# Talking-heads attention feeding a gated feed-forward on one core: two score tiles per step, and the last two batches' attention values kept in SBUF

## The chip, the cores and the metric

One core of a Trainium2 chip runs the whole program. The metric is device time in microseconds (us), the median of three executions; lower is better. Beside it stands one profiled execution, from which all durations below come.

## The reference, cut to what matters

```python
# attention: q, k, v are (4 batches, 12 heads, 448 tokens, 64), float32
scores = scale * np.matmul(q, k.transpose(0, 1, 3, 2))
scores = np.einsum('bhij,hg->bgij', scores, w_pre)        # heads mixed before the softmax
scores = scores - np.max(scores, axis=-1, keepdims=True)
attn = np.exp(scores)
attn = attn / (np.sum(attn, axis=-1, keepdims=True) + 1e-09)
attn = np.einsum('bhij,hg->bgij', attn, w_post)           # and after it
attn_out = np.matmul(attn, v)
# x is attn_out as (1792 tokens, 768); the feed-forward has d_ff = 1536
g = x @ w_gate
out = (g * (1.0 / (1.0 + np.exp(-g))) * (x @ w_val)) @ w_out
```

The three feed-forward weights come in as float64 and are turned into float32 on the chip.

## The kernel before, in words

**Stages.** The attention of batches 0 to 3 runs first, and the feed-forward after it in two halves: first the tokens of batches 2 and 3, then those of batches 0 and 1. For the second half the products of the two batches are combined from seven sums and differences of their values (`b11`, `t1`, `b21` and so on), which the attention of batch 1 makes (`second_values`, L379, with `operand`, L355) and stores in DRAM.

**Attention of a batch.** `load_k`, `kprep`, `kcopy` bring and transpose the keys, two heads at a time (six steps); `load_q`, `qprep`, `qcopy` the queries, 128 rows at a time (four chunks, two steps each). `qk` (L207) makes the scores of a group of head pairs, `qkcopy` (L220) copies them from PSUM to the tile `stg`, and `store` (L229) sends them to DRAM (`s_d`). There are 21 such groups in a batch: six for each of three chunks and three for the last. Rows are then worked in 45 tiles of ten query rows (`NTB`), two tiles making a unit (`NUB` = 23 units, the last with one tile). For each unit `gather` (L247) reads the scores of its rows back from DRAM with heads on the partitions, and `pre` (L264) mixes the heads into two PSUM banks, one for each tile. For each tile follow `top` (L276, row maximum, VectorE), `expo` (L282, exponential and row sum, ScalarE), `norm` (L288, reciprocal on VectorE, then the scaled mixing weights `rw` on GpSimd), `post` (L296, second mixing, eight matmuls) and `mixed` (L307, copy into the ring `attnT`, ScalarE). `av` (L317) multiplies by the values for two heads and two column chunks of 112 rows; `values` (L332) splits the result into a high and a low part (ScalarE copy, VectorE subtraction). For batches 2 and 3 both parts go to DRAM as `x_d`, and `load_x` and `load_last` (L667, L673) read them back into the two large tiles `x0`, `x1` before the feed-forward's first products (`up`, L679).

**PSUM.** The eight banks are four pairs: `qk`, `pre`, `post`, and `tr` for transposes and `av`. A `pre` bank is free again when its tile's `expo` has read it.

**Order.** It is written by hand. Every step is entered with `at(key, step)`, and `run` (L86) issues all steps in the order of their keys; each engine and each DMA queue works through its own steps in that order. A key counts tiles: batch b begins at `n0 = 45*b`, unit u at `n0 + 2*u`; I call the stretch of two tiles from there a slot. Nearly all DMAs go through the SP queue, which holds what is behind a DMA that still waits. From key 163.2 (`START`) the first three weight units are converted to float32 during the attention (`convert`, eight steps, seven of them on VectorE for these units), and the feed-forward's own keys start at `END` = 192.

```python
at(n + 0.5, later(pre, b, u))                          # L447, n = n0 + 2*u
n = n0 + t - x + 0.5                                   # L450, x = t % 2
at(n + 0.3 + 0.1 * x, later(top, b, t))
at(n + 0.9 + 0.4 * x, later(expo, b, t))
at(n + 1.6 + 0.4 * x, later(norm, b, t))
at(n + 2.7 + 0.8 * x, later(post, b, t))
at(n + 3.2 + 0.8 * x, later(mixed, b, t))
```

## Time and profile before

| what | us |
|---|---|
| median of three executions (1033.2 to 1205.98) | 1034.08 |
| the profiled execution | 1040.06 |
| its span, from first to last instruction | 1038.3 |
| TensorE busy (its matmuls) | 989.4 |
| VectorE busy | 670.3 |
| ScalarE busy | 432.5 |
| GpSimd busy | 229.5 |

The profile has a page with busy times, and views that answer questions: a timeline (start, duration, engine, line, operation, tile; in brackets the idle time of the engine in front of it and what ended it), a table of busy time by stretch, and a list of waits. PE is TensorE's matmuls, PEld its weight loads, DVE VectorE, ACT ScalarE, POOL GpSimd, SPq the DMAs that the SP queue issues. The ends of matmuls are modelled in these rows and overlap with the next ones, so what a step takes from TensorE is read here from the start of one group to the start of the next.

### The profile page before, as it was taken

The page shows a single profiled execution, that of the slowest core. Times are in us where ns is not written, and L with a number is a line of the kernel's source. Part 1 is how long each engine was busy: PE and PEld are TensorE (multiplying, and loading weights), DVE is VectorE, ACT ScalarE, POOL GpSimd, SP SyncE. Part 2 cuts the span into 40 slices and gives each one's busy share as a digit, 9 for nine tenths or more (in the row PEclk, how much of TensorE's full clock was granted, in tenths as well). Part 3 has the DMA queues.
Part 4 walks back from the last instruction along what each step waited for, and adds up shares of the span by engine and source line. Part 5 has one row for each costly group of instructions (what it writes and reads, how often), then busy time and mean ns, then how long its engine had stood idle before and what let it go on. Part 6 is the DMA issues. An engine that isn't in the chain of part 4 may idle for free.

```text
span 1038.3 us, 18515 instructions
## 1 busy us (share of the span) xinstructions
PE 989.4 (95%) x6732; PEld 770.9 (74%) x6732; DVE 670.3 (65%) x1336; ACT 432.5 (42%) x961; POOL 229.5 (22%) x278
## 2 busy tenths in 40 slices
PE   5899999989989999999969999999999999999998
PEld 2456556645545665556859999999999899999998
DVE  3466555656556655547459999999954999994110
ACT  1355555644545555555523333332313444442110
POOL 2011111101101111112223443344413333330000
PEclk9799999989999999999989999999999999999999
DMA  7789776987679965787745454557974111111311
GB/s 193 237 223 280 230 220 209 286 235 246 191 234 273 272 219 182 222 245 228 242 144 183 156 164 147 173 164 250 325 246 150 61 62 61 61 61 62 104 45 36
DMA packets 159318, 190.05 MB, mean 183 GB/s; under 512 B 56984, under 2 KB 134652, under 8 KB 159228
## 3 DMA queue, kind: packets, MB, share of 16 engines
q1 hardware_dynamic: 158972, 188.78, 59.7%
q8 instruction: 54, 0.88, 0.4%
q14 instruction: 36, 0.29, 0.1%
q0 software_dynamic: 256, 0.09, 0.0%
HBM read 114.10 MB, written 74.75 MB: 182 GB/s over the span
## 4 chain that ended last, share of the span: by engine, by line
PE 72%; DVE 14%; DMA 6%; ACT 3%; issue 2%; POOL 2%; SPq 1%; ACTq 0%; DVEq 0%; POOLq 0%
PE post L302 13%; PE pre L272 9%; PE qk L217 7%; PE av L324 6%; PE dn L721 6%; PE dn L722 6%; PE dn L723 6%; PE p L619 4%; PE p L622 4%; PE p L620 4%; DVE w L540 2%; DVE w L542 2%; DVE stg L225 1%; DVE wlo L558 1%; DMA raw<-in_moe_w_val_dram 1%
## 5 line engine op out<-in xcount | busy, mean ns | idle before, releaser
L302 PEld LDWEIGHTS post<-rw,e 128*112 128x112 f32 x1440 | 160.2, 179 | 83.8 <-issue 49.6
L302 PE MATMUL post<-rw,e 128*112 128x120 f32 (+1 forms) x1440 | 187.1, 277 | 5.9 <-POOL rw L293 5.3
L293 POOL TENSOR_SCALAR rw<-w_post_gs,st 128x120 f32<-128x120 f32 x180 | 69.1, 387 | 425.4 <-DVE st L291 249.4
L285 ACT ACTIVATE e<-pre,st 128x448 f32<-128x448 f32 x180 | 114.0, 633 | 97.2 <-DVE st L279 97.2
L279 DVE TENSOR_REDUCE st<-pre 128x1 f32<-128x448 f32 x180 | 105.0, 619 | 67.2 <-PE pre L272 62.5
L721 PE MATMUL dn<-whi,gh 128*128 128x256 f32 x504 | 141.6, 281 | 1.4 <-DVE u L626 1.4
L723 PE MATMUL dn<-whi,gl 128*128 128x256 f32 x504 | 141.5, 281 | 0.0
L722 PE MATMUL dn<-wlo,gh 128*128 128x256 f32 x504 | 141.4, 281 | 0.0
L530 POOL TENSOR_SCALAR mag<-mag 128x768 f32<-128x768 f32 x33 | 98.9, 2997 | 150.1 <-ACT mag L528 147.3
L272 PE MATMUL pre<-rs,w_pre_blocks 60*64 60x448 f32 x720 | 116.9, 581 | 15.3 <-ACT e L285 11.6
L311 ACT ACTIVATE attnT<-post 112x480 f32<-112x480 f32 (+3 forms) x192 | 103.1, 545 | 34.2 <-PE post L302 33.7
L721 PEld LDWEIGHTS dn<-whi,gh 128*128 128x128 f32 x504 | 95.0, 188 | 1.6 <-DVE u L626 1.6
L722 PEld LDWEIGHTS dn<-wlo,gh 128*128 128x128 f32 x504 | 95.0, 189 | 0.0
L723 PEld LDWEIGHTS dn<-whi,gl 128*128 128x128 f32 x504 | 95.0, 188 | 0.0
L225 DVE COPY stg<-qk 128x448 f32<-128x448 f32 x124 | 73.2, 618 | 27.4 <-PE qk L217 26.9
L217 PE MATMUL qk<-kk,qt 64*128 64x448 f32 (+1 forms) x384 | 89.9, 605 | 0.8 <-ACT stg L227 0.6
L324 PE MATMUL av<-attnT,vn 112*64 112x224 f32 (+1 forms) x864 | 84.9, 342 | 2.3 <-DVE xs L338 1.9
L324 PEld LDWEIGHTS av<-attnT,vn 112*64 112x64 f32 x864 | 54.6, 139 | 28.7 <-issue 8.3
L558 DVE TENSOR_TENSOR wlo<-w,whi 128x768 fp32r<-128x768 f32 x48 | 45.6, 952 | 30.5 <-ACT whi L562 30.2
L272 PEld LDWEIGHTS pre<-rs,w_pre_blocks 60*64 60x64 f32 x720 | 25.8, 133 | 51.6 <-ACT e L285 33.0
L686 PE MATMUL upg<-x,whi 128*128 128x448 f32 x144 | 54.2, 376 | 6.9 <-DMA x<-x_d 6.9
L562 ACT ACTIVATE whi<-w 128x768 fp32r<-128x768 f32 x48 | 40.1, 839 | 37.2 <-PE dn L723 21.6
(115 smaller groups left out, 1647.6 us busy)
## 6 DMA issues: line engine op xcount, KB each, us to landing
rs<-s_d SPq DMA_DIRECT2D x176, 210.0 KB, 4.4
s_d<-stg SPq DMA_DIRECT2D x72, 448.0 KB, 3.6
w_d<-w SPq DMA_DIRECT2D x36, 384.0 KB, 2.7
w<-w_d SPq DMA_DIRECT2D x36, 384.0 KB, 3.3
raw<-in_moe_w_gate_dram SPq DMA_DIRECT2D x12, 768.0 KB
raw<-in_moe_w_val_dram SPq DMA_DIRECT2D x12, 768.0 KB, 4.8
raw<-in_moe_w_out_dram SPq DMA_DIRECT2D x12, 768.0 KB, 5.5
kn<-in_k_dram SPq DMA_DIRECT2D x24, 224.0 KB, 5.7
```

The source lines that it names most:

```text
L217: nc.tensor.matmul(pt[x][i * m:(i + 1) * m], qt[b, c][hs, p, :m], kk[b, p][hs], start=True, stop=True)
L225: nc.vector.tensor_copy(stg[b, c, g][:, x], pt)
L272: nc.tensor.matmul(pt[r][x * HB:(x + 1) * HB], wpre[i], xs[i, x], start=True, stop=True)
L279: nc.vector.tensor_reduce(st[:, 0:1], pt, axis=AX.X, op=ALU.max, negate=True)
L285: nc.scalar.activation(e, pt, AF.Exp, bias=st[:, 0:1], scale=1.0, accum_out=st[:, 1:2])
L302: nc.tensor.matmul(pt[:, c, :, :m], e[:, c * CP:(c + 1) * CP], w[:, :, :m], start=True, stop=True)
L311: nc.scalar.activation(attnT[:, :, :, i:i + m].rearrange("p c h i -> p (c h) i"), pt[:, :, :, done:done + m].rearrange("p c h i -> p (c h) ...
L324: nc.tensor.matmul(pt[j * D:(j + 1) * D], vn[b][:, 2 * p + j, c], ring[:, c, 2 * p + j, segs[0]:segs[-1] + 1:max(1, segs[-1] - segs[0])], ...
L530: eng.tensor_scalar(mag, mag, f32_of(0x38000000), f32_of(0x47EFFFFF), op0=ALU.max, op1=ALU.min)
L721: nc.tensor.matmul(pt, gh, hi, start=opens, stop=False)
L722: nc.tensor.matmul(pt, gh, lo, start=False, stop=False)
L723: nc.tensor.matmul(pt, gl, hi, start=False, stop=closes)
```

## The change

1. **Two tiles together.** `top`, `expo`, `post`, `mixed` of the two tiles of a unit stand directly behind one another, both `expo` ahead of the `mixed` of the unit before, and `norm` works once for a unit: one addition and one reciprocal on two columns, then two `rw` on GpSimd. Both `post` (16 matmuls) stand together.
2. **All attention steps by slots.** One scoring group, with its copies and its store, stands in each slot; key and query preparation, `av`, `values` have fixed places in a slot. Of the second query chunk of batch 0 only the first group's products stand in front of the first `pre` (before, four groups did). In batch 0 both first query loads are entered behind the six key loads and ahead of the score stores.
3. **Batches 2 and 3 straight into SBUF.** `values` writes the high and low parts into `x0` and `x1`; `x_d`, its 30 stores and 16 loads go.
4. **Batch 1's sums.** The low parts of `t1` to `t4` and one subtraction move from VectorE to GpSimd (30 operations of 128x224), the steps stand later, and for the second pair later still. Buffers: `xs` 4 for 3, `x_b12` 2 for 1.
5. **Start of the feed-forward.** The whole first gate product and the first half of the first value product stand ahead of the last six `av`.

```diff
-    xsp = pool(right, "xsp", 3, "right")
+    xsp = pool(right, "xsp", 4, "right")
...
-        early_bank = b == 0 and c < 2 and g % 2 and g < 5
+        early_bank = b == c == 0 and g % 2 and g < 5
...
+    def norm(b, u):
+        n = len(tiles_of(u))
+        st = sts.pop((b, u))
+        nc.vector.tensor_scalar(st[:, 2, :n], st[:, 1, :n], 1e-9, None, op0=ALU.add)
+        nc.vector.reciprocal(st[:, 2, :n], st[:, 2, :n])
+        for r, t in enumerate(tiles_of(u)):
+            w = rw[b, t] = smp.tile([P, H, TS], F32, tag="rw", name=f"rw_{b}_{t}")
+            nc.gpsimd.tensor_scalar(w, wpost, st[:, 2, r:r + 1], 1.0, op0=ALU.mult, op1=ALU.mult)
...
         if b * S >= TB:
-            keep_x(x_d[:, p * P:(p + 1) * P, ts], xs, m)
+            if (0, 0) not in xs_:
+                for x in range(2):
+                    xs_[0, x] = stp.tile([P, NKC, TB], F32R, tag="stg", name=f"x{x}")
+            hi, lo = (xs_[0, x][:, p, ts].rearrange("p (s i) -> p s i", s=m) for x in range(2))
...
+            eng = nc.vector if order else nc.gpsimd
             for o, i in order or [(slice(None), slice(None))]:
-                nc.vector.tensor_tensor(xs[:, 1, i], src[:, o], xs[:, 0, i].bitcast(F32), op=ALU.subtract)
+                eng.tensor_tensor(xs[:, 1, i], src[:, o], xs[:, 0, i].bitcast(F32), op=ALU.subtract)
...
-            nc.vector.tensor_tensor(xt["b21", c], xt["b21", c], xt["t1"], op=ALU.subtract)
+            nc.gpsimd.tensor_tensor(xt["b21", c], xt["b21", c], xt["t1"], op=ALU.subtract)
...
+    BACK = 13
+        def slot(u):
+            return (n0 if u >= 0 else n0 - NTB) + 2 * (u if u >= 0 else u + NUB)
...
+            n = slot(BACK - 2 + p - NUB) if b else (-31.8 + 0.5 * p if p < 2 else -31.8 + p)
+            at(n - 4 if b else -60 + p, later(load_k, b, p))
+            at(n + 1.25, later(kprep, b, p))
+            at(n + 1.45, later(kcopy, b, p))
...
+            if b:
+                at_k = [slot(BACK - NUB + done + g) for g in range(len(groups(c)))]
+                ready = [slot(BACK - NUB + done - (4 if c == 0 else 2) + g) for g in range(2)]
+            elif c == 0:
+                at_k, ready = [-29.65 + g for g in range(NPAIR)], [-32.3, -30.8]
+            elif c == 1:
+                at_k, ready = [-1.0 + 1.2 * g for g in range(NPAIR)], [-5.0, -4.0]
             else:
+                at_k = [slot(done - 9 + g) for g in range(len(groups(c)))]
+                ready = [slot(done - 11 + g) for g in range(2)]
+            at(min(ready[0] - 8, -54 + c) if b == 0 and c < 2 else ready[0] - 8, later(load_q, b, c))
...
+            for g, n in enumerate(at_k):
+                at(n + 0.65, later(qk, b, c, g))
                 for x in range(2):
+                    at(n + (0.9 if x or g % 2 else 1.1), later(qkcopy, b, c, g, x))
+                at(n + 1.4, later(store, b, c, g))
+            done += len(at_k)
         for u in range(NUB):
+            n = slot(u)
+            at(n - 4.05, later(gather, b, u))
             at(n + 0.5, later(pre, b, u))
+            for t in tiles_of(u):
+                x = 0.02 * (t % 2)
+                at(n + 0.6 + x, later(top, b, t))
+                at(n + 0.95 + x, later(expo, b, t))
+                at(n + 3.2 + x, later(post, b, t))
+                at(n + 3.5 + x, later(mixed, b, t))
+            at(n + 1.25, later(norm, b, u))
...
+            first = (-(-(c0 + m) * CP // TS) - 1) // 2 + 2
             for p in range(NPAIR):
+                u = first + (max(0, p - 1) if m == 2 else p // 2)
+                if u < NUB:
+                    n = slot(u)
+                elif b < B - 1:
+                    n = n0 + NTB + 2 * (u - NUB)
+                else:
+                    n = n0 + NTB + 2.0 + 0.3 * p
+                n += 0.01 * p
                 if b != 1:
+                    at(n + 1.3, later(av, b, c0, m, p))
+                    at(n + 1.9, later(values, b, c0, m, p))
                     continue
...
+                for step, y in enumerate((1.9, 2.3, 2.5, 2.9)):
+                    at(n + y + (0.7 if p == 1 else 0), later(second_values, c0, m, x, step))
...
-            for c in range(NKC):
-                at(B * NTB - 9.6 + 1.2 * c, later(load_x, 0, c))
-                at(B * NTB - 2.8 + 0.9 * c, later(load_x, 1, c))
-            for x in range(2):
-                at(B * NTB + 2.6 + 0.5 * x, later(load_last, x, 0, 3 * CP))
-                at(B * NTB + 9.7 + 0.1 * x, later(load_last, x, 3 * CP, S))
...
-                    at(B * NTB + UPH, later(up, b, f, "g", hf, True, False))
-                    at_ff(n, later(up, b, f, "g", hf, False, True))
+                    at(B * NTB + 1.0, later(up, b, f, "g", hf))
+                    at(B * NTB + 2.3, later(up, b, f, "v", hf, True, False))
+                    at(B * NTB + 5.0, later(up, b, f, "v", hf, False, True))
```

## Rows read from the trace of the kernel before

**Rows 1.** Busy table: us of PE, PEld, DVE, ACT, POOL; clock, DMA share, GB/s.

```profile
35.60:150.50 114.90, 111.84 (x794) 65.71 (x794) 67.33 (x195) 62.59 (x164) 16.97 (x47) 0.96 0.84 243
150.50:276.40 125.90, 118.09 (x881) 70.19 (x880) 72.56 (x219) 68.31 (x191) 16.22 (x45) 0.96 0.81 237
276.40:397.70 121.30, 115.61 (x877) 69.03 (x876) 72.69 (x219) 66.32 (x179) 16.69 (x45) 0.99 0.82 242
397.70:509.90 112.20, 109.37 (x893) 69.50 (x892) 66.52 (x188) 63.36 (x163) 19.19 (x44) 0.98 0.72 214
509.90:529.20 19.30, 10.51 (x121) 8.86 (x120) 7.96 (x15) 6.05 (x12) 5.66 (x2) 0.85 0.81 254
```

**Rows 2.** Timeline, PE, batch 0, both tiles' second mixing together; columns start, duration.

```profile
129.51 1.54 PE L272 MATMUL pre<-rs,w_pre_blocks 60*64 60x448 f32 x8
130.98 1.02 PE L217 MATMUL qk<-kk,qt 64*128 64x448 f32 x4
131.93 1.90 PE L302 MATMUL post<-rw,e 128*112 128x120 f32 x16
133.76 1.50 PE L272 MATMUL pre<-rs,w_pre_blocks 60*64 60x448 f32 x8
```

**Rows 3.** Timeline, PE, batch 2, a stretch without waits.

```profile
343.29 0.98 PE L272 MATMUL pre<-rs,w_pre_blocks 60*64 60x448 f32 x8
344.20 1.74 PE L324 MATMUL av<-attnT,vn 112*64 112x224 f32 x16
345.87 1.08 PE L302 MATMUL post<-rw,e 128*112 128x120 f32 x8
346.78 0.55 PE L175 MATMUL ktr<-ident,kn 112*128 112x112 f32 x4
347.16 0.58 PE L302 MATMUL post<-rw,e 128*112 128x120 f32 x4
```

**Rows 4.** Timeline, three engines, softmax steps behind the first `pre` of rows 2.

```profile
131.16 1.16 DVE L279 TENSOR_REDUCE st<-pre 128x1 f32<-128x448 f32 x2 [0.76 <-PE pre L272]
131.88 0.63 ACT L285 ACTIVATE e<-pre,st 128x448 f32<-128x448 f32 x1 [1.40 <-DVE st L279]
...
133.05 0.57 ACT L311 ACTIVATE attnT<-post 112x480 f32<-112x480 f32 x1 [0.44 <-PE post L302]
...
133.51 0.63 ACT L285 ACTIVATE e<-pre,st 128x448 f32<-128x448 f32 x1
...
134.28 0.20 PEld L272 LDWEIGHTS pre<-rs,w_pre_blocks 60*64 60x64 f32 x6 [0.34 <-ACT e L285]
```

**Rows 5.** Waits between 52 and 520 us: total us, times, longest.

```profile
ACT xs_t L359 <- DMA x_t<-xs_t: 9.1, 2, 5.6
```

**Rows 6.** Timeline, the start: SP queue issues and the first `pre`.

```profile
1.24 6.12 SPq L163 DMA_DIRECT2D kn<-in_k_dram  x6
...
11.26 8.75 SPq L233 DMA_DIRECT2D s_d<-stg  x6
...
30.86 1.14 SPq L253 DMA_DIRECT2D rs<-s_d  x2
...
35.60 2.59 PE L272 MATMUL pre<-rs,w_pre_blocks 60*64 60x448 f32 x8 [3.43 <-DMA rs<-s_d]
```

**Rows 7.** Busy table, two stretches in which the granted clock falls.

```profile
35.20:45.40 10.20, 9.80 (x32) 4.00 (x33) 5.42 (x14) 2.17 (x6) 0.71 (x2) 0.50 0.97 304
...
520.00:546.00 26.00, 17.77 (x89) 16.22 (x90) 14.02 (x22) 4.72 (x8) 5.76 (x2) 0.80 0.47 140
```

**Rows 8.** Timeline, PE, the feed-forward's first gate product, its two token halves.

```profile
507.01 0.37 PE L686 MATMUL upg<-x,whi 128*128 128x448 f32 x1
507.21 0.36 PE L687 MATMUL upg<-x,wlo 128*128 128x448 f32 x1
...
529.21 0.74 PE L686 MATMUL upg<-x,whi 128*128 128x448 f32 x1 [6.90 <-DMA x<-x_d]
```

**Rows 9.** One tile's operations on GpSimd: durations in ns, smallest, median, largest.

```profile
L595 POOL TENSOR_TENSOR ss<-w,w x12: 1022/1282/1618, 779.6 to 923.4; 128x384 f32<-128x384 f32 x12
```

More of the change, by code (lines that the diff above doesn't have):

```diff
@@ L50, in talking_heads_moe_kernel @@
     dram = ctx.enter_context(tc.tile_pool(name="dram", bufs=1, space=bass.MemoryType.DRAM))
-    x_d = dram.tile([2, NKC * P, TB], F32, name="x_d")
     x_o = {x: dram.tile([2, DM // 2, S], F32, name=f"x_{x}") for x in ("b11", "b21", "b22", "t1", "t2", "t3", "t4")}
@@ L208, in qk @@
         m = scored(c)
-        early_bank = b == 0 and c < 2 and g % 2 and g < 5
+        early_bank = b == c == 0 and g % 2 and g < 5
         pt = [
-            ps.tile([P, S], F32, tag=("pre" if c == 0 else "post") if early_bank else "qk", name=f"qk_{b}_{c}_{g}_{x}")
+            ps.tile([P, S], F32, tag="pre" if early_bank else "qk", name=f"qk_{b}_{c}_{g}_{x}")
             for x in range(2)
@@ L333, in values @@
         pt, order = avs.pop((b, c0, p))
[L334 to L338 removed]
         ts = slice(b * S % TB + c0 * CP, b * S % TB + (c0 + m) * CP)
         if b * S >= TB:
[L341 removed]
+            if (0, 0) not in xs_:
[3 more added lines that the diff above has]
+        else:
+            xs = xsp.tile([P, 2, 2, CP], F32R, tag="xs", name=f"xs_{b}_{c0}_{p}")[:, :, :m]
+            hi, lo = xs[:, 0], xs[:, 1]
+        for o, i in order:
+            nc.scalar.activation(hi[:, i], pt[:, o], AF.Copy)
+        for o, i in order:
+            nc.vector.tensor_tensor(lo[:, i], pt[:, o], hi[:, i].bitcast(F32), op=ALU.subtract)
+        if b * S >= TB:
             return
@@ L422, in talking_heads_moe_kernel @@
         for p in range(NPAIR):
-            n = n0 + SCORE - 2.5 + QSTEP * p if b else (-30.5 + 0.5 * p if p < 2 else -30.5 + p)
-            at(n - 5 if b else -60 + p, later(load_k, b, p))
-            at(n, later(kprep, b, p))
-            at(n + 0.3, later(kcopy, b, p))
-        for c in range(NQ):
-            if (b, c) == (0, 0):
-                load, ready, step = -61, -31, 1.0
-                score = -29.0
-            else:
-                step = QSTEP
-                score = n0 + SCORE + step * NPAIR * c
-                load, ready = score - 10, score - 4
-            at(load, later(load_q, b, c))
-            for g in range(2):
-                at(ready + 1.5 * g, later(qprep, b, c, g))
-                at(ready + 1.5 * g + 0.4, later(qcopy, b, c, g))
-            for g in range(len(groups(c))):
-                at(score + step * g, later(qk, b, c, g))
+            n = slot(BACK - 2 + p - NUB) if b else (-31.8 + 0.5 * p if p < 2 else -31.8 + p)
@@ L441, in talking_heads_moe_kernel @@
                 for x in range(2):
-                    at(score + step * g + 0.4, later(qkcopy, b, c, g, x))
-                at(score + step * g + 0.9, later(store, b, c, g))
+                    at(n + (0.9 if x or g % 2 else 1.1), later(qkcopy, b, c, g, x))
+                at(n + 1.4, later(store, b, c, g))
+            done += len(at_k)
         for u in range(NUB):
-            n = n0 + 2 * u
-            at(n - 4.6, later(gather, b, u))
+            n = slot(u)
+            at(n - 4.05, later(gather, b, u))
@@ L447, in talking_heads_moe_kernel @@
             at(n + 0.5, later(pre, b, u))
-        for t in range(NTB):
-            x = t % 2
-            n = n0 + t - x + 0.5
-            at(n + 0.3 + 0.1 * x, later(top, b, t))
-            at(n + 0.9 + 0.4 * x, later(expo, b, t))
-            at(n + 1.6 + 0.4 * x, later(norm, b, t))
-            if b == B - 1 and t >= NTB - LAG:
-                n += min(1.0, (NTB - 1 - t) / 4.0)
-            at(n + 2.7 + 0.8 * x, later(post, b, t))
-            at(n + 3.2 + 0.8 * x, later(mixed, b, t))
+            for t in tiles_of(u):
[4 more added lines that the diff above has]
+                at(n + 3.5 + x, later(mixed, b, t))
@@ L463, in talking_heads_moe_kernel @@
                 if b != 1:
-                    at(n, later(av, b, c0, m, p))
-                    at(n + 0.6, later(values, b, c0, m, p))
+                    at(n + 1.3, later(av, b, c0, m, p))
+                    at(n + 1.9, later(values, b, c0, m, p))
                     continue
@@ L487, in talking_heads_moe_kernel @@
     EARLY = 3
-    raws, cvs, w32, wsp, xs_, ups, sgs, ms, g_, yps = ({} for _ in range(10))
+    raws, cvs, w32, wsp, ups, sgs, ms, g_, yps = ({} for _ in range(9))
     def unit_shape(u):
@@ L665, in gated_high @@
         nc.scalar.activation(g_[b, f][0][:, hf * S:(hf + 1) * S], ms[hf], AF.Copy)
-    def load_x(x, c):
-        if c == 0:
-            xs_[0, x] = stp.tile([P, NKC, TB], F32R, tag="stg", name=f"x{x}")
-        nc.sync.dma_start(out=xs_[0, x][:, c, :S].bitcast(F32), in_=x_d[x, c * P:(c + 1) * P, :S])
-    def load_last(x, t0, t1):
-        ts = slice(S + t0, S + t1)
-        nc.sync.dma_start(
-            out=xs_[0, x][:, :, ts].bitcast(F32), in_=x_d[x, :, ts].rearrange("(c p) t -> p c t", p=P)
-        )
     def up(b, f, nm, hf, high=True, low=True):
```

62 lines of the change are left out of this document (25 added, 37 removed).

## The prediction

> **What bounds the kernel now.** I read three views in this order: the busy table, cut at the first `pre` of each batch; PE's timeline in single slots; then the other engines' timeline where PE waited. The busy table has PE at work nearly always during the attention, 111.84 of 114.90 us in batch 0 [rows 1]. A busy PE is no proof that the time is needed, so I price the work by the start of one group to the start of the next, where nothing waits: `pre` 343.29 to 344.20 is 0.91 us, an `av` 1.67, the `post` of one tile 0.91, four key transposes 0.38 [rows 3]; a scoring group is 0.95 (130.98 to 131.93) and the `post` of two tiles 1.83 [rows 2]. A batch has 23 `pre` (20.9), 22 double `post` and a single one (41.2), 21 scoring groups (20.0), 12 `av` (20.0) and 14 transposing steps (5.3, the queries' taken as the keys'): 107.4 us. Batches 1 and 2 took 125.9 and 121.3 [rows 1]. So PE is the bound, but 14 to 18 us of a batch are waiting, most of it inside rows that call PE busy.
>
> One such wait shows in the timeline: `pre` held PE for 1.47 us (129.51 to 130.98), not 0.91 [rows 2]. The maxima of both tiles were done by 132.3, but ScalarE had the `mixed` of the earlier unit in its order between the two exponentials; that waited for `post`, so the second exponential ran at 133.51 and ended at 134.14, and the next `pre` got its second bank only then [rows 4].
>
> The Trainium skill takes a side between the two readings (Perfetto Trace Analysis, Identifying the Most-Contended Engine): matmul busy time does not tell the headroom, the busy share of the weight loads does. The trace bears it out: weight loads were busy for 65.71 of the 114.90 us [rows 1]. Read by the matmul column alone, the sum would be that of the first rival below.
>
> **The change, part by part.**
>
> *Two tiles together, and slots.* With both `expo` ahead of `mixed`, the second exponential follows the first. From the end of `pre` (131.06) the two maxima take until 132.32; the first exponential starts at 131.88, and the second can follow some 0.8 us later, the 0.63 and the reading of the sum between: about 132.7 to 133.3, 2.2 us behind `pre` [rows 4]. Meanwhile PE has a scoring group and a double `post`, 0.95 + 1.83 = 2.78 us [rows 2]. The wait goes, with 0.5 us to spare. What is late next is `rw`: addition, reciprocal and two GpSimd operations end some 1.5 us later, 3.8 behind `pre` (an estimate from rows 4), and the `post` that needs them stands behind the next `pre` and scoring group, at 2.78 + 0.91 + 0.95 = 4.6. It is covered too. One addition and reciprocal fewer a unit on VectorE, which has room, costs and brings nothing.
>
> So each batch can come near its own sum. Batch 0 has six `av` less (10.0) and, as the slots place them, three scoring groups more (2.9): 100.3 against 114.9, 14.6 over. Batch 1: 18.5 over; batch 2: 13.9. Batch 3: 20.9 + 41.2, 11 scoring groups 10.5, 12 `av` 20.0, six of half the columns at half (5.0), four transposing steps 1.5, and the first twelve matmuls of the gate product, in its stretch before and after, at 0.20 each (507.01 to 507.21 [rows 8]) 2.4: 101.5 against 112.2, 10.7 over [rows 1]. Together 57.7 us. Not all goes:
>
> - The clock was 0.50 for 10.2 us from 35.20 [rows 7], behind an idle start that stays: 5.1 us kept.
> - Slots 11 and 12 of every batch have no scoring group: 1.83 us of cover for the 2.2. 0.4 us, eight times: 3 us.
> - Batch 1's sums. ScalarE stood up to 5.6 us for an `xs` buffer whose store had not gone out [rows 5], and PE behind it. A fourth buffer and later steps should end the long ones; I keep 0.5 us in each of the ten slots with such sums: 5 us.
> - Batch 3's weight conversions stay in VectorE's order between the maxima. Half of its excess: 5 us. Seams between batches: 2 us.
>
> Kept 20 us (8, if only the first two stay; 40, if each is double), gained 37.7.
>
> *GpSimd's share.* A 128x384 operation took 1.02 to 1.62 us there [rows 9]; for 224 columns that is 0.6 by columns and 1.62 at most. I take 0.75, the median's share. The costliest slot has four of them and two `rw`: under 4 us of a slot of 0.91 + 0.95 + 1.83 + 1.67 = 5.4. Hidden; at 1.62 each it would be 7.2, nearly 2 us late in six slots, 11 us, which is in the range.
>
> The Trainium skill speaks against this edit (GPSIMD Engine Reference, Engine selection): two-input elementwise work belongs on VectorE, GpSimd being about twice as slow. By its factor the operations would still lie inside the slot, and the sum would be the same.
>
> *The start.* The first query load now stands behind the six key loads, whose issue takes 6.12 us, so the six stores, which went out until 20.0, go out until about 26.1. Before, the first `gather` stood in the SP queue behind two stores of the second chunk, until 30.86; now none of these is in front of it. With 3 us for the stores to land (an estimate; 4.7 at most, as the `gather` itself took to 35.60) the first `pre` comes at 33.8 to 35.5 [rows 6]. I take 1.8 us of gain; from below nothing.
>
> *The end of the attention.* From the last `post` at 509.9 to 529.20 PE had 10.51 us of work and 8.8 idle [rows 1], waiting at the end for `x0`, `x1` from DRAM (6.90 us, [rows 8]); the clock was down on average to 0.80 of 26 us [rows 7], and the next twelve matmuls at half speed cost 0.20 more each, 2.4. Without `x_d` only the last copy and subtraction stand between `av` and the product: 1 us by the sizes of rows 4 (0 to 4, when VectorE is behind). Gain 8.8 + 2.4 − 1.0 = 10.2. The 46 DMAs that vanish free the SP queue; I cost that at nothing.
>
> **Sum.** 37.7 + 1.8 + 10.2 = 49.7 us. The profiled execution takes 1040.06 (span 1038.3, 1.8 around it); it would take 990.4. The median of the runs is 6.0 lower, 1034.08, and comes to 984.4, so 984. Bounds: 49.7 + 12 + 1 makes 971, and 966 with half of the cold start gone as well; 40 kept, no gain at the start, 7.2 at the end make 1034 − 24.9 = 1009.
>
> **Rivals.**
>
> *PE's busy time is work.* Then only its idle time can go: 3.1 + 7.8 + 5.7 + 2.8 = 19.4 us in the four batches [rows 1]. A quarter of it stays, and 12.0 come from the start and the end: 1034 − 14.5 − 12.0 = 1008; with most of the idle time kept, 1018. For it speaks that the first columns are nearly full; against it the same `pre` at 1.47 and 0.91 us [rows 2, 3].
>
> *The SP queue holds the gathers.* In batch 1 three stores of a slot wait for GpSimd's results, and the `gather` of a later unit stands behind them. It has 4.55 keys of lead, 2.3 slots or 12 us of these slots, of which 4.7 are the transfer; the mechanism decides once GpSimd is over 7 us late. Then ten slots wait up to 4.7 us: 984 + 47 = 1031. The 1.62 us of rows 9 speak for it, the slot's spare time against.
>
> *DMA is the bound.* Batch 0 moved 243 GB/s [rows 1]; in 100.3 us the same bytes would need 278. If 243 were the ceiling, little of the attention's gain would come: about 1022. The 304 GB/s of [rows 7] speak against it.
>
> *The softmax chain outlasts its cover (slower).* Both `expo` of a unit now run behind both maxima, and the next `pre` needs both. If VectorE's two score copies or a `mixed` come in between, the 2.2 us grow by 0.6 to 1.7, up to 3.9 against 2.78: 1.1 us in each of 90 slots, 99 us, in place of the 52.6 that waits cost beyond the cold start: 1034 + 99 − 52.6 − 12.0 = 1068. It decides from 0.7 us a slot, that is from a chain of 3.5 us. The order of the keys speaks against it: copies and `mixed` come behind both `expo`.
>
> *Direct values bring nothing,* since the products then wait for weights that VectorE has not converted: 984 + 10 = 994, inside the range.
>
> **How the numbers follow.** My forecast has 0.70, with the last rival in it, and its own range is 966 to 1009; busy time is work 0.14; SP queue 0.07; DMA 0.03; the slower one 0.06. The range of 966 to 1018 holds the first two but for a part, 0.81. About 2% (under 1013, over 1055) is what a measurement of this kernel can tell from no change. Faster: 0.70, and 0.07 of the 1008 to 1018 case: 0.77. Slower: 0.06. Same: the rest, 0.17.
>
> **What would show it.** PE's timeline in slots 6 to 12: `pre` to `pre` 3.7 to 4.1 us with `post` in sixteens and `pre` at 0.91. Batch stretches of about 104, 113, 110 and 107 us. The first `pre` near 34. No wait for `x` ahead of the feed-forward, and under 12 us from the last `post` to the second half of the gate product. Wrong: a `pre` still at 1.4 us (the chain), PE idle for `rs` (DMA or SP), `post` waiting for `rw` in batch 1's sums (GpSimd), the first product halves waiting for `wlo` (conversions).

## The result, and the profile after

The changed kernel takes 996.69 us (median of four executions, 991.94 to 997.15), the kernel before 1038.43 beside it: a ratio of 0.961, with a 95% interval of 0.9548 to 0.9673. Of the kernel before one execution was slow (1205.98 us), and one of e8 below (1063.43 us, at a mean clock of 0.85); the medians 1038.43 and 1003.56 count them, the ratios do not. The forecast was 984, with a range of 966 to 1018. The profiled execution took 991.94 us (span 990.2), against 1040.06 before: 48.1 us less, where the sum of the forecast came to 49.7.

One thing has to be put right first. The cuts of [rows 1] are not the first `pre` of each batch: from batch 1 on they lie one unit later (counted by the eight matmuls of a unit, the first `pre` of batch 1 is at 145.44, not 150.50). The sum over the batches is not touched by that; the single stretches are. This is the kernel before with the right cuts, in the columns of [rows 1]; the last row of those stands as it was:

```profile
35.60:145.44 109.84, 108.30 (x765) 63.19 (x765) 64.06 (x184) 60.25 (x158) 15.92 (x44) 0.95 0.85 246
145.44:271.28 125.84, 118.03 (x879) 70.14 (x877) 72.56 (x219) 68.31 (x191) 16.22 (x45) 0.96 0.81 237
271.28:393.20 121.92, 115.70 (x878) 69.07 (x876) 72.49 (x219) 66.32 (x179) 16.73 (x45) 0.99 0.81 238
393.20:509.90 116.70, 112.89 (x923) 72.03 (x922) 69.97 (x199) 65.70 (x169) 20.20 (x46) 0.99 0.73 216
```

and this the changed kernel, cut at the same events:

```profile
31.90:137.78 105.88, 103.42 (x785) 62.05 (x785) 62.36 (x147) 60.90 (x160) 15.62 (x45) 0.98 0.92 261
137.78:251.03 113.25, 108.79 (x877) 67.64 (x876) 63.01 (x160) 67.73 (x191) 25.51 (x61) 1.00 0.91 263
251.03:363.25 112.22, 109.36 (x878) 67.65 (x877) 63.00 (x160) 65.37 (x179) 25.57 (x61) 1.00 0.86 247
363.25:473.99 110.74, 105.76 (x924) 70.12 (x923) 65.61 (x154) 64.89 (x170) 23.18 (x47) 1.00 0.63 187
473.99:482.88 8.89, 8.89 (x117) 7.97 (x117) 1.64 (x6) 3.90 (x9) 0.00 (x0) 1.00 0.27 90
```

The reader sees three gains: 3.7 us at the start (35.60 to 31.90), 32.2 over the four batches (4.0, 12.6, 9.7 and 6.0), and 10.4 from the last `post` to the gate product's second half (19.30 to 8.89). The other 1.8 lie behind it. The borders blur 1.2 us: six more matmuls of the gate product, at 0.20, now stand in front of the last `post`, so batch 3 gained 7.2 by its own work and the end 9.2. The clock column tells a part of the second gain: the length of a stretch by what the clock lacks to 1.00 makes about 13 us before (0.95, 0.96, 0.99, 0.99) and 2 now (0.98, then 1.00). Behind four waits of 1.7 to 3.9 us in batches 1 to 3 the kernel before ran at a clock of 0.50 for 3.4 to 6.8 us (from 226.40, 250.30, 304.90 and 468.70); the changed kernel has no such stretch there, though one wait of 2.3 us is left in it (at 215.60).

A slot without other work, of TensorE and ScalarE, to be laid beside [rows 2] and [rows 4] (start, duration):

```profile
60.95 0.98 PE L270 MATMUL pre<-rs,w_pre_blocks 60*64 60x448 f32 x8
...
61.86 1.02 PE L216 MATMUL qk<-kk,qt 64*128 64x448 f32 x4
...
62.77 0.63 ACT L287 ACTIVATE e<-pre,st 128x448 f32<-128x448 f32 x1 [0.99 <-DVE st L281]
62.81 1.90 PE L306 MATMUL post<-rw,e 128*112 128x120 f32 x16
...
63.39 0.63 ACT L287 ACTIVATE e<-pre,st 128x448 f32<-128x448 f32 x1
...
64.00 0.57 ACT L315 ACTIVATE attnT<-post 112x480 f32<-112x480 f32 x1
...
64.64 0.98 PE L270 MATMUL pre<-rs,w_pre_blocks 60*64 60x448 f32 x8
```

`pre` takes 0.91 us, the second exponential follows the first by 0.62 and ends 0.62 before the next `pre` (64.02 to 64.64), and the slot takes 3.69. The end of the attention, to be laid beside [rows 8]:

```profile
470.40 1.38 PE L701 MATMUL upg<-x,whi 128*128 128x448 f32 x6
473.14 1.03 PE L306 MATMUL post<-rw,e 128*112 128x96 f32 x8 [1.36 <-POOL rw L298]
473.95 0.45 PE L696 MATMUL upv<-x,whi 128*128 128x448 f32 x1
...
476.55 5.07 PE L328 MATMUL av<-attnT,vn 112*64 112x112 f32 x96
481.55 1.48 PE L701 MATMUL upv<-x,whi 128*128 128x448 f32 x6
482.88 0.36 PE L696 MATMUL upg<-x,whi 128*128 128x448 f32 x1
```

Behind the last `post`, which itself waited 1.36 us for `rw`, no wait is left: the high half of a value product stands in front of the last `av`, its low half behind, and covers ScalarE's copies and VectorE's subtractions.

### The profile page after: what moved, and what is told of

Same layout as the page of the kernel before. It is cut to its first block, busy times and chain, and to the rows that moved or that the text cites. A ratio compares the mean times of both kernels' runs of the same rounds, so it can differ in the third digit from the quotient of the medians.

```text
span 990.2 us, 18171 instructions
## 1 busy us (share of the span) xinstructions
PE 951.3 (96%) x6732; PEld 757.2 (76%) x6732; DVE 642.2 (65%) x1130; ACT 429.1 (43%) x961; POOL 248.1 (25%) x308
## 4 chain that ended last, share of the span: by engine, by line
PE 84%; DMA 7%; DVE 3%; ACT 2%; SPq 2%; POOL 1%; issue 1%; ACTq 0%; POOLq 0%; DVEq 0%
PE post L306 13%; PE pre L270 7%; PE qk L216 7%; PE dn L731 6%; PE dn L733 6%; PE dn L732 6%; PE av L328 6%; PE p L641 5%; PE p L644 5%; PE p L642 5%; DMA rs<-s_d 3%; PE upv L701 3%; PE upv L696 3%; PE upv L697 3%; PE upg L701 3%; PE upg L696 3%
## 5 line engine op out<-in xcount | busy, mean ns | idle before, releaser
L306 PEld LDWEIGHTS post<-rw,e 128*112 128x112 f32 x1440 | 153.7, 177 | 65.9 <-issue 42.7
L306 PE MATMUL post<-rw,e 128*112 128x120 f32 (+1 forms) x1440 | 170.8, 272 | 6.1 <-POOL rw L298 3.8
L270 PE MATMUL pre<-rs,w_pre_blocks 60*64 60x448 f32 x720 | 101.3, 565 | 11.1 <-DMA rs<-s_d 8.4
L315 ACT ACTIVATE attnT<-post 112x480 f32<-112x480 f32 (+3 forms) x192 | 97.0, 550 | 13.3 <-PE post L306 9.1
L216 PE MATMUL qk<-kk,qt 64*128 64x448 f32 (+1 forms) x384 | 87.9, 583 | 3.9 <-DVE stg L223 1.9
L328 PE MATMUL av<-attnT,vn 112*64 112x224 f32 (+1 forms) x864 | 81.6, 336 | 0.0
L216 PEld LDWEIGHTS qk<-kk,qt 64*128 64x128 f32 (+1 forms) x384 | 26.8, 174 | 57.3 <-issue 35.4
L687 ACT ACTIVATE gh<-m 128x448 fp32r<-128x448 f32 x36 | 20.9, 579 | 76.3 <-DVE m L712 68.9
```

Source lines behind the costliest of these rows:

```text
L216: nc.tensor.matmul(pt[x][i * m:(i + 1) * m], qt[b, c][hs, p, :m], kk[b, p][hs], start=True, stop=True)
L270: nc.tensor.matmul(pt[r][x * HB:(x + 1) * HB], wpre[i], xs[i, x], start=True, stop=True)
L306: nc.tensor.matmul(pt[:, c, :, :m], e[:, c * CP:(c + 1) * CP], w[:, :, :m], start=True, stop=True)
L315: nc.scalar.activation(attnT[:, :, :, i:i + m].rearrange("p c h i -> p (c h) i"), pt[:, :, :, done:done + m].rearrange("p c h i -> p (c h) ...
L328: nc.tensor.matmul(pt[j * D:(j + 1) * D], vn[b][:, 2 * p + j, c], ring[:, c, 2 * p + j, segs[0]:segs[-1] + 1:max(1, segs[-1] - segs[0])], ...
```

## The experiments

Times are medians; "before" in a ratio is the kernel before on the same chip. The changed kernel's own interval is 13 us wide, so a difference of 4 to 6 us from it is likely at best, not clear of noise.

| run | us | ratio to before (95%) |
|---|---|---|
| changed kernel | 996.69 | 0.961 (0.9548 to 0.9673) |
| e1 order of before | 1006.24 | 0.9694 (0.9652 to 0.9736) |
| e2 values by DRAM | 1009.45 | 0.9714 (0.9680 to 0.9748) |
| e3 sums on VectorE | 997.38 | 0.9595 (0.9567 to 0.9623) |
| e4 gathers earlier | 995.54 | 0.9588 (0.9564 to 0.9612) |
| e5 pairs alone | 1014.07 | 0.9769 (0.9744 to 0.9793) |
| e6 query first | 992.70 | 0.9572 (0.9550 to 0.9595) |
| e7 loads spread | 990.07 | 0.9543 (0.9509 to 0.9577) |
| e8 conversions in slots | 1003.56 | 0.9650 (0.9627 to 0.9672) |
| e9 late `rw` on VectorE | 997.22 | 0.9621 (0.9597 to 0.9645) |
| e10 = e7, stores later | 995.74 | 0.9613 (0.9593 to 0.9633) |
| e11 = e6 + e7 + e9 + e10 | 988.70 | 0.9531 (0.9515 to 0.9547) |
| e12 = e6 + e7 + fifth buffer | 980.40 | 0.9448 (0.9415 to 0.9481) |

### What the two tiles together are worth: e1 and e5

e1 undoes ScalarE's order alone (`x` is 0.02 for the second tile, so its `expo` comes at n + 1.6, behind a `mixed` at n + 1.5):

```diff
-                at(n + 0.95 + x, later(expo, b, t))
+                at(n + 0.95 + 32.5 * x, later(expo, b, t))
-                at(n + 3.5 + x, later(mixed, b, t))
+                at(n + 3.5 + 15 * x, later(mixed, b, t))
-            at(n + 1.25, later(norm, b, u))
+            at(n + 1.7, later(norm, b, u))
```

> The changed kernel, but the second exponential of a unit stands behind the first `mixed` of the unit before it, as before the change, and `norm` behind it; everything else as changed. Theory (the order on ScalarE was the wait): in the slots without `av`, about twelve a batch, `pre` goes from 0.91 us back to about 1.45, with the same 0.34 us wait of the weight load for `e` in front of its second bank; in slots with `av` the 1.67 us more of TensorE work hide it. That is 48 slots by 0.55: 26 us, so 1012 to 1030. Rival (it was the even placing of scoring groups and `av` that gave the gain, the order nothing): `pre` stays near 0.91 and the time within 5 us of the changed kernel's 996.7.

Measured: 1006.24, 9.5 us more than the changed kernel; in the profiles the attention takes 452.6 us and not 441.2. The wait came back as described, on ScalarE and TensorE:

```profile
60.95 0.57 ACT L315 ACTIVATE attnT<-post 112x480 f32<-112x480 f32 x1
...
61.42 0.63 ACT L287 ACTIVATE e<-pre,st 128x448 f32<-128x448 f32 x1
...
61.66 1.50 PE L270 MATMUL pre<-rs,w_pre_blocks 60*64 60x448 f32 x8
...
63.09 1.02 PE L216 MATMUL qk<-kk,qt 64*128 64x448 f32 x4
```

`pre` takes 1.43 us (61.66 to 63.09) and the slot 4.21, 0.52 more than 3.69. Neither expectation holds in its sum, though. Some fourteen slots pay the whole 0.52; key and query transposes hide all but some 0.2 in about as many others, and `av` all of it. And 4.3 of the 11.3 us are those of a single slot in batch 1's sums, where ScalarE waited for an `xs` buffer, as it did in other runs too. The order alone is worth 7 to 11 us.

e5 puts the whole pairing into the kernel before; besides, the last batch's `post` lose a delay of up to one key that they had there:

```diff
+            at(n + 1.25, later(norm, b, u))
...
-            at(n + 0.9 + 0.4 * x, later(expo, b, t))
-            at(n + 1.6 + 0.4 * x, later(norm, b, t))
...
-            at(n + 2.7 + 0.8 * x, later(post, b, t))
-            at(n + 3.2 + 0.8 * x, later(mixed, b, t))
+            at(n + 0.95 + x, later(expo, b, t))
+            at(n + 3.2 + x, later(post, b, t))
+            at(n + 3.5 + x, later(mixed, b, t))
```

> The kernel before, with the first part of the change alone: both maxima, both exponentials, one `norm`, both `post` and both `mixed` of a unit stand together, at the keys of the changed kernel; scoring groups, preparation, `av` and everything else stay where they were. Theory (the two tiles together are worth most of the attention's 32 us): ScalarE's order 10 us, as its undoing cost in e1, and the seam of a second `post` 10 us more, since one `post` by itself takes 1.00 us in the trace of before and one of a pair 0.91, for 116 of them: minus 20, about 1017; the slots are then worth the other 12. Rival 1 (without the slots a pair of `post` stands at times with no scoring group in front, and waits for `rw`): minus 5 or less, over 1032. Rival 2 (the slots are worth nothing): minus 32, about 1005.

Measured: 1014.07, 24 us less than before. The attention, first `pre` to last `post`, takes 444.4 us in the profile, against 473.5 before and 441.2 in the changed kernel: the pairing brings 29.0 of the 32.2 us, the slots and the rest 3.2, though the changed kernel's stretch holds 4.1 us more of work (three scoring groups and the six gate matmuls). Of the 29, ScalarE's order is 7 to 11, if it is worth the same here as in e1. Another part is at `post`. Alone it costs more than in a pair, as in the kernel before (TensorE):

```profile
320.43 1.02 PE L217 MATMUL qk<-kk,qt 64*128 64x448 f32 x4
321.38 1.08 PE L302 MATMUL post<-rw,e 128*112 128x120 f32 x8
322.38 0.98 PE L272 MATMUL pre<-rs,w_pre_blocks 60*64 60x448 f32 x8
```

1.00 us by itself (0.91 in front of transposes, [rows 3], as 24 of them stand), 1.83 for two (62.81 to 64.64 above): a seam of 0.09, for 116 single ones an estimated 8 to 10 us. A single `post` also stood at times directly behind `pre` and waited for its `rw`; that the other 8 to 14 us are this wait was not shown by a run.

But e5's gain ends at 24, not 29, for the end of the attention grew: from the last `post` to the gate product's second half it takes 23.1 us, against 20.2 before. Its two waits are 10.9 us together, 1.90 and 6.90 before; that batch 3, now faster, gives the values' way through DRAM less cover fits this, but was not tested. TensorE in e5:

```profile
495.23 1.64 PE L330 MATMUL av<-attnT,vn 112*64 112x112 f32 x16 [4.84 <-DVE xs L344]
502.91 0.74 PE L690 MATMUL upg<-x,whi 128*128 128x448 f32 x1 [6.04 <-DMA x<-x_d]
```

### The values straight into SBUF: e2

```diff
-            hi, lo = (xs_[0, x][:, p, ts].rearrange("p (s i) -> p s i", s=m) for x in range(2))
...
+            keep_x(x_d[:, p * P:(p + 1) * P, ts], xs, m)
...
+                at(B * NTB - 9.6 + 1.2 * c, later(load_x, 0, c))
+                at(B * NTB - 6.8 + 0.9 * c, later(load_x, 1, c))
...
+                at(B * NTB + 9.7 + 0.1 * x, later(load_last, x, 3 * CP, S))
```

> The changed kernel, but the values of batches 2 and 3 go to DRAM and are read back into the two large tiles, as before the change (the loads of the low part stand four keys earlier than then). Theory (the way through DRAM was the wait at the end of the attention): from the last `post` to the second half of the gate product it takes 16 to 20 us again, not 9, with a wait of 5 us or more for `x` from DRAM: plus 7 to 11 us, 1004 to 1008. Rival (with the other steps regular the way is hidden, or the weights would be waited for anyway): plus 2 us at most.

Measured: 1009.45, 12.8 us more. TensorE in e2, behind the low half of the value product:

```profile
487.89 1.49 PE L708 MATMUL upv<-x,whi 128*128 128x448 f32 x6
497.65 0.74 PE L703 MATMUL upg<-x,whi 128*128 128x448 f32 x1 [8.28 <-DMA x<-x_d]
498.20 0.57 PE L704 MATMUL upg<-x,wlo 128*128 128x448 f32 x1
498.57 0.57 PE L703 MATMUL upg<-x,whi 128*128 128x448 f32 x1
```

The wait for `x` is 8.28 us, longer than the 6.90 of [rows 8], and the matmuls behind it come every 0.37 us, not every 0.20: the clock is at 0.50. From last `post` to gate product it is 18.3 us against 9.7, as the theory had it. So in the profiles 8.6 us lie here, and 3.1 behind. The rest is spread over the attention, most of it in batch 2 (116.2 us, 112.2 in the changed kernel); that the stores to DRAM cost it there is not shown. By the ratios (0.9714 and 0.961) the part is worth about 11 us, near the forecast's 10.2.

### GpSimd's share of the sums: e3

```diff
-            eng = nc.vector if order else nc.gpsimd
+            eng = nc.vector
...
-            nc.gpsimd.tensor_tensor(xt["b21", c], xt["b21", c], xt["t1"], op=ALU.subtract)
+            nc.vector.tensor_tensor(xt["b21", c], xt["b21", c], xt["t1"], op=ALU.subtract)
```

> The changed kernel, but all low parts of the sums of batch 1, and the subtraction that makes `t4`, on VectorE, as before the change; their later places and the fourth buffer stay. Theory (the engine does not matter, the places and buffers do): within 2 us of the changed kernel, 994 to 999; batch 1 takes 113 us as with GpSimd. Rival (VectorE's queue was the wait): the maxima come later in the ten slots with sums, `e` waits for `st` there by half a microsecond to one more, plus 5 to 10 us, all of it in batch 1.

Measured: 997.38, no difference. On GpSimd the 30 operations took 0.66 us each (0.75 was taken), on VectorE 0.38 to 0.40; the engine for them does not matter to the total, as costed. Batch 1 took 115.7 us in e3's profile, not 113; with the sums on GpSimd it took 112.9 to 114.9 in e4, e8 and e9.

### The start: e6

```diff
-            at(min(ready[0] - 8, -54 + c) if b == 0 and c < 2 else ready[0] - 8, later(load_q, b, c))
+            at((-61, -53)[c] if b == 0 and c < 2 else ready[0] - 8, later(load_q, b, c))
```

> The changed kernel, but the first query load of batch 0 is entered ahead of the six key loads, as before the change; the second stays behind them. Theory (the first query chunk, landed at 11.9 us, is what the stores of the first chunk wait for): the first query transpose goes from 12.0 to about 5 us, the stores end near 20 and not 25.4, the first `pre` comes at 26 to 28 and not 31.9: minus 4 to 6 us, 991 to 993. Rival (the keys, or the DMA engines, set the stores' times anyway, or the start at half clock grows by what is gained): the first `pre` at 30 or later, or within 1.5 us of the changed kernel's time.

Measured: 992.70, 4 us less, the lower edge of the theory, though the executions of the two overlap (991.53 to 998.31, and 991.94 to 997.15). SP's queue in the changed kernel and then in e6:

```profile
6.09 2.84 SPq L152 DMA_DIRECT2D qn<-in_q_dram  x2
17.36 8.35 SPq L231 DMA_DIRECT2D s_d<-stg  x6
...
28.68 2.64 SPq L251 DMA_DIRECT2D rs<-s_d  x6
```

```profile
0.72 0.44 SPq L152 DMA_DIRECT2D qn<-in_q_dram  x1
...
11.05 9.28 SPq L231 DMA_DIRECT2D s_d<-stg  x6
...
23.27 2.64 SPq L251 DMA_DIRECT2D rs<-s_d  x6
```

The first `pre` comes at 26.33, not 31.90. Not all of these 5.6 us arrive: in this profile batches 0 to 2 took 1.7 to 2.0 us longer each. The query load behind the keys was a loss inside a change that won here all the same, since the `gather` no longer stands behind the second chunk's stores.

### What the batches still wait for: e4, e7, e10, e12

In slots 11 to 13 of each batch TensorE still waited for `rs`, and in batch 1's sums ScalarE for `xs`. e4 enters the gathers a slot earlier (the first line of the diff), e7 the value loads two and the key loads one slot earlier as well, with three `kn` buffers for two:

```diff
-            at(n - 4.05, later(gather, b, u))
+            at(n - (4.05 if b == 0 and u < 7 else 6.05), later(gather, b, u))
-            at(n0 + 16.9 + 1.95 * c, later(load_v, b, c))
+            at(n0 + 12.9 + 1.95 * c, later(load_v, b, c))
-            at(n - 4 if b else -60 + p, later(load_k, b, p))
+            at(n - 6 if b else -60 + p, later(load_k, b, p))
```

> The changed kernel, but each `gather` from unit 7 on, and all of the later batches, stands one slot earlier in the SP queue (key n - 6.05 for n - 4.05); same buffers. Theory (the lead of two slots is too short where loads of keys and values share the DMA engines, slots 10 to 13): the waits of `pre` for `rs`, 1.1 to 1.5 us in each batch, and what `pre` loses right behind them go: minus 4 to 8 us, 989 to 993. Rival (the DMA engines are full there, so nothing lands earlier in the end): the wait moves to a neighbouring slot, within 1.5 us of the changed kernel.

> The changed kernel with the loads of slots 8 to 14 spread: each `gather` one slot earlier (as in e4), the four value loads of a batch two slots earlier, the key loads of the next batch one slot earlier with a third buffer for them. In e4 the wait for `rs` had gone and TensorE waited 1.0 to 1.2 us for the keys instead. Theory (it is the crowd of keys, values and gathers at one time that comes late, not the sum of a batch's transfers): both waits go, minus 4 to 8 us, 989 to 993. Rival (the DMA engines have no slack over a whole batch): a wait for `rs` or keys stays somewhere in each batch, within 1.5 us of the changed kernel.

Measured: e4 995.54, no gain; e7 990.07, 6 to 7 us less (in the profiles batches 1 to 3 are 1.6, 0.6 and 1.7 us shorter). The waits between 52 and 470 us (total, times, longest), of the changed kernel:

```profile
ACT xs_t L369 <- DMA x_t<-xs_t: 12.2, 7, 4.4
...
PE pre L270 <- DMA rs<-s_d: 4.1, 4, 1.5
```

of e4:

```profile
PE ktr L174 <- DMA kn<-in_k_dram: 3.6, 4, 1.2
```

and of e7:

```profile
ACT xs_t L369 <- DMA x_t<-xs_t: 9.4, 3, 5.8
...
PE pre L270 <- DMA rs<-s_d: 0.9, 1, 0.9
```

In e4 the 4.1 us of waiting for `rs` had become 3.6 of waiting for keys: a crowd of loads, in which who stands in front decides who is late. Spread out, both go, but for 0.9.

What stayed in e7 is the stall of ScalarE. SP's queue and ScalarE, and the busy table's row with the clock behind it:

```profile
206.97 3.73 SPq L231 DMA_DIRECT2D s_d<-stg  x1
...
212.78 0.38 SPq L361 DMA_DIRECT2D x_t<-xs_t  x1
```

```profile
216.34 0.39 ACT L369 ACTIVATE xs_t<-xb 128x224 fp32r<-128x224 f32 x1 [5.83 <-DMA x_t<-xs_t]
```

```profile
217.60:221.00 3.40, 3.40 (x20) 3.38 (x18) 2.32 (x6) 2.75 (x9) 0.80 (x2) 0.50 0.69 227
```

ScalarE waits 5.83 us for a buffer whose store went out late; TensorE stands 3.7 us for `attnT` behind it, and then runs 3.4 us at half clock. I took the score store that held SP for 3.73 us for the cause, and moved such stores behind the next slot's copies (e10, on e7):

```diff
-                at(n + 1.4, later(store, b, c, g))
+                at(n + (2.9 if b else 1.4), later(store, b, c, g))
```

> The kernel of e7 (gathers, values and keys spread), but from the second batch on the store of a scoring group stands 1.5 keys later in the SP queue, behind the next slot's score copies. In e7 such a store held the SP queue for 3.73 us from 206.97, the store of a sum behind it went out at 212.78 only, ScalarE waited 5.83 us for that buffer, and TensorE stood 3.7 us; the same in batch 2 at 282. Theory (the queue held by a store that is not ready is what makes batch 1's sums stall): both stalls, 5.0 and 4.2 us with what follows them, shrink to a third, minus 4 to 8 us against e7's 990.1: 982 to 986. Rival (the sums' stores land late because the DMA engines are full, or ScalarE's own order sets it): the stall stays near 212 us, within 2 us of e7.

Measured: 995.74, worse than e7, and the stall was there still. The theory fell: in e10 it is a pair of gathers that holds SP,

```profile
209.83 4.36 SPq L251 DMA_DIRECT2D rs<-s_d  x2
214.29 0.38 SPq L361 DMA_DIRECT2D x_t<-xs_t  x1
```

without a releaser in the trace, while the DMA share is over 1.0 by the profile (1.18 from 208 to 212). Nor had e7's store waited for its data: the copies for it had ended at 202.32. In the attention of e7 and e10 all five SP issues of over 2.7 us stand where the share is 1.18 to 1.25; that they wait until earlier transfers land is my reading, which no run tested. If the transfer can't be had earlier, what waits for it can be taken away: a fifth buffer (e12, on e6 and e7 together; `rw` has three buffers and not four, for the space):

```diff
-    xsp = pool(right, "xsp", 4, "right")
+    xsp = pool(right, "xsp", 5, "right")
```

> The edits of e6 (first query load first) and e7 (loads spread), without those of e9 and e10, and a fifth buffer for `xs` in place of the fourth; for its space `rw` has three buffers and not four. In e7 and e10 the fifth operand of the first two pairs of batch 1 waited 5.8 and 6.5 us for the store of the first, whose issue stood behind transfers that the SP queue could not hand on while the DMA share was over 1.0 by the profile. Theory (that buffer is what ties ScalarE to the DMA engines): the wait of ScalarE for `xs` shrinks from 9 to 10 us over batch 1's sums to under 3, the stall near 212 us and the one near 280 go, batches 1 and 2 take 107 to 109 us: with e6's 4 and e7's 6 us, 978 to 983. Rival (with a fifth buffer the next thing that needs the DMA engines waits, `rs`, keys or the values read back): about the sum of e6 and e7 alone, 986 to 990.

Measured: 980.40, inside the theory's 978 to 983. The waits of e12 and its busy table for batches 1 and 2:

```profile
ACT xs_t L369 <- DMA x_t<-xs_t: 5.3, 2, 4.8
```

```profile
133.83:241.37 107.54, 106.97 (x877) 67.16 (x876) 63.30 (x160) 67.62 (x191) 25.57 (x61) 1.00 0.94 271
241.37:350.01 108.64, 107.67 (x877) 67.29 (x876) 63.30 (x160) 65.55 (x179) 25.57 (x61) 1.00 0.90 263
```

One wait of 4.8 us is left on ScalarE, now in a place where `av` covers most of it (the two slots there take 1.2 us more than two without a wait); the expected "under 3" was too low. Both batches come to within 0.1 and 1.2 us of the 107.4 that the forecast had counted as their work. e12 beats both kernels, by 56 and 16 us. e6 and e7 together without the fifth buffer were not run; by their single gains that would be about 986.

### The last batch: e8, e9, e11

In the last batch `post` waited for `rw`, four times over 0.5 us. e8 spreads the weight conversions, from slot 11 on, two of VectorE's steps a slot, right behind `norm` (`i` is the unit, 0 to 2; the weights' loads, stores and splits move along):

```diff
-    START = (B - 1) * NTB + 28.2
+    START = (B - 1) * NTB + 22.0
...
+                s0 = (B - 1) * NTB
...
+                    o = 7 * i + step - 1
+                    n = s0 + 26 + 2 * (o // 2) + 1.3 + 0.01 * (o % 2)
...
+                    at(n, later(convert, u, step))
```

> The changed kernel, but the conversion of the first three weight units starts in slot 11 of the last batch and not in slot 14, and VectorE's seven steps of each stand two a slot, directly behind `norm`. Theory (conversions between the maxima hold up `rw` and so `post`): the waits of `post` for `rw` in the last batch, 1.2 to 1.5 us each at about 437, 456, 464 and 470 us in the changed kernel, go: the last batch takes 105 and not 110 us, minus 3 to 6, 991 to 994. Rival (ScalarE or the chain of `values` sets them): the waits stay or move, within 1.5 us of the changed kernel.

Measured: 999.03 to 1003.95 in the four executions that its ratio counts, about 5 us worse; both expectations fell. The groups of GpSimd's `rw` (busy us, mean ns) show that the operation got slower, not faster: the changed kernel from 31 to 400 us, the same from 415 to 480, and e8 from 415 to 480:

```profile
L298 POOL TENSOR_SCALAR rw<-w_post_gs,st 128x120 f32<-128x120 f32 x149 | 52.5, 365 | 284.8 <-DVE st L295 151.7 <-PE post L306 129.6 <-PE ktr L174 3.4
```

```profile
L298 POOL TENSOR_SCALAR rw<-w_post_gs,st 128x120 f32<-128x120 f32 x23 | 12.4, 551 | 41.3 <-DVE st L295 30.9 <-PE av L328 7.4 <-PE pre L270 3.0
```

```profile
L298 POOL TENSOR_SCALAR rw<-w_post_gs,st 128x120 f32<-128x120 f32 x25 | 17.3, 704 | 43.0 <-DVE st L295 39.0 <-PE pre L270 4.0
```

The same operation takes 365 ns in the mean, 551 while VectorE converts between other steps, and 704 where the conversions stand right in front of it. One by one, e8's nine that began while no conversion ran took 363 to 369 ns, the sixteen others 496 to 1847. The Trainium skill has the rule (SBUF — State Buffer, Who interferes with whom): GpSimd and part of VectorE's instructions use one shared pair of ports, an exclusive lock, and whoever comes second stands still. The trace agrees, with 496 ns at the least against 369. But this is not what made e8 slower: in its profile `post` waited less for `rw` in the last batch (1.8 us in all, not 3.8), and that batch is only 0.6 us longer. The feed-forward behind it is 3.7 us longer, and the start stays longer at half clock; both differ nearly as much between runs whose steps there are the same (see the median, below), so where the 5 us come from stays open. e9 takes `rw` away from GpSimd there:

```diff
-            nc.gpsimd.tensor_scalar(w, wpost, st[:, 2, r:r + 1], 1.0, op0=ALU.mult, op1=ALU.mult)
+            eng = nc.vector if b == B - 1 and u >= 11 else nc.gpsimd
+            eng.tensor_scalar(w, wpost, st[:, 2, r:r + 1], 1.0, op0=ALU.mult, op1=ALU.mult)
```

> The changed kernel, but from unit 11 of the last batch on the two `rw` of a unit are made on VectorE, directly behind the reciprocal, and not on GpSimd. In e8 the conversions stood right behind `norm` and the waits for `rw` did not go: two `rw` then took up to 2.32 us on GpSimd, against 0.71 where VectorE converted nothing. Theory (GpSimd and VectorE get into each other's way while VectorE converts, and that makes `rw` late): a pair of `rw` takes under 0.6 us, the waits of `post` for it at about 437, 456, 464 and 470 us in the changed kernel shrink to 0.3 or less, the last batch takes 105 to 107 and not 110 us: minus 3 to 5, 991 to 994. Rival (the exponentials, or VectorE's queue of conversions, set the time of `rw` on any engine): waits for `rw` of about 1 us remain, within 1.5 us of the changed kernel.

Measured: 997.22, no gain. `rw` took 281 ns on VectorE, and of the waits for it one of 0.5 us was left, nearly as the theory had it; but `attnT`, `x` and `e` were waited for in their place, and the last batch's profile is only 1.6 us shorter. The late `rw` was real and not what sets this stretch.

> The changed kernel with the edits of e6 (first query load first), e7 (loads spread), e9 (late `rw` of the last batch on VectorE) and e10 (stores later) together. If each brings what it should by itself and they add up: first `pre` at 26 to 28 (minus 4), batches of 106, 107, 107 and 104 us: 972 to 980. If the edits only pass the same waits on to one another, as e4 did: 986 or more.

Measured: 988.70. The sum of the single gains was not reached, as e10's edit is a loss and e9's nothing. e12 leaves these two out, but also adds the buffer, so it does not show what they cost.

## Why the prediction came out as it did

**What bounds the kernel: right.** Work priced by start to start, 107.4 us for a batch, is what e12 comes down to (107.54 and 108.64); that nothing goes below it is not shown. Had PE's busy time been work, the first rival, batch 1 could not have gone under 118. The rule of the Trainium skill that the prediction set against the trace (Perfetto Trace Analysis, Identifying the Most-Contended Engine) did not help further: the weight loads' busy share was 56% in batch 1 of the kernel before (70.14 of 125.84) and is 62% in e12 (67.16 of 107.54), which is within 0.1 us of the summed work; by itself it does not tell the two apart.

**The chain: right in kind and size, in fewer slots.** 2.2 us of softmax behind 2.78 of cover: the second `e` ends 0.62 before the next `pre`, where 0.5 was worked out. Its undoing costs 0.52 a slot, but 7 to 11 us in all. As much again, an estimated 8 to 10 us, came from both `post` standing together, which the sum contained (22 pairs at 1.83) and the text never named; 8 to 14 us of the pairing's 29 have no cause shown.

**What was kept: 24.3 us, not 20.** The stretches less their work: 5.6, 5.9, 4.8 and 8.0 us. (The sum took twelve gate matmuls into batch 3's work; eighteen stand in its stretch, 1.2 us more.) The start's half clock took 6.8 us, not 10.2, so 3.4 and not 5.1. Slots 11 and 12 did lose, but to gathers that came late, not to the chain: a wait for DMA that the prediction had only under the heading of what would prove it wrong, and which cost 4.1 us. Batch 1's sums were sized about right, but reach into batch 2, which lost 4.8 us with 0.8 and seams reckoned. Batch 3 lost 8.0 and not some 6; e8 and e9 did not bring it back, so its cause stays open.

**The start: gain of 3.7, not 1.8.** The gathers were issued at 28.68 (about 29.1 worked out, 26.1 and 3), but landed after 3.2 us, where the sum took the 4.7 of [rows 6].

**The end: 9.2 and 1.8 behind it, not 10.2.** Of the 1.0 us between `av` and product nothing is seen; the value product covers it. The next twelve matmuls, at half clock before, now come every 0.20 us.

**The median: the step that failed.** The sum missed the profiled execution by 1.6 us. The other 11 of the 12.7 us between 984 and 996.69 come from the last step, which took over the 6.0 us by which the old kernel's median lay under its profiled execution. The new one's lies 4.8 above. That offset belongs to one execution and not to the kernel. Of the old 6.0, two to four came from a median of only three executions: four later medians, of eleven each, are 1036.13 to 1038.0. For the new 4.8, runs with the same steps show how far profiles differ. The start at half clock lasted as long in e3 and e9 as here, but twice as long in e4, e7 and e8:

```profile
29.90:36.70 6.80, 4.49 (x12) 1.09 (x12) 1.44 (x3) 1.34 (x4) 0.00 (x0) 0.50 0.86 249
```

```profile
29.90:43.60 13.70, 11.12 (x37) 5.00 (x38) 4.77 (x11) 3.69 (x10) 0.72 (x2) 0.50 0.83 246
```

(the changed kernel, then e7). Batch 0 took 105.9 to 106.9 us in the first three and 108.6 to 109.6 in the others. The unchanged feed-forward, from the gate product's second half on, took 505.9 us (e7) to 510.7 (e3), 507.3 in the changed kernel. So it is partly luck that the sum met the profile so closely: 991.94 is the fastest of the changed kernel's executions, and by the ratio and its interval the change is worth about 40 us of 1037 (34 to 47), not 48.1.

**The rivals.** That SP's queue holds the gathers did not happen as described, but a relative did: in e7 and e10 it was SP's queue that held the sums' stores. DMA as the bound fell: batch 1 of the changed kernel moved 263 GB/s and e12's 271. The slower case fell: no slot of the changed kernel shows that chain.

## What to carry to other kernels

Price a busy engine's work from start to start in a clean stretch; the sum that comes out is a mark that further edits can be aimed at. A wait for a transfer in a crowded stretch is passed on when one transfer is moved ahead, and goes when the crowd is spread, or stops costing when the consumer gets one buffer more. The difference between one profiled execution and a median is no term of a forecast, and a sum that meets a single profile is not yet shown right.

## What the runs showed of the hardware that I had not expected

- A stall of 3.7 us on TensorE is followed by 3.4 us at a granted clock of 0.50, so by the clock it costs 1.7 us more than it lasts (e7, at 217.60). The same start of the program is followed by 6.8 us at half clock in the profiles of the changed kernel, e3 and e9, by 10.2 in e2 and e10, and by 13.7 in e4, e7 and e8.
- SP's issue of a single DMA took 3.73 and 3.90 us where the DMA share was 1.2, with no releaser in the trace (e7 at 206.97, e10 at 209.83), and everything behind it in the queue went out later.
- `rw` on GpSimd takes 363 to 369 ns, and 496 to 1847 when it starts while VectorE converts (e8).
- Eight matmuls between others of another kind take 1.00 us, sixteen together 1.83.
